# The last token tile in two feature halves, its rows stored alone, its stores from two queues

## The chip, the cores and the metric

The kernel runs on one core of one Trainium2 chip. The metric is device time in microseconds (us), the median over runs. It is 0.6 ms here, and the change touches its last 10 us, so besides the time of the whole program this document uses a second measure, the **tail**: from the start of the first matmul of the last token tiles (called t0; the first instruction that writes the tile `po` at the end) to the end of the span. The tail is worked out from each profile as span minus t0, with the span to three decimals from the trace and t0 to two, so a tail can be off by 0.01.

In the profile lines PE is TensorE (matmuls), DVE VectorE, ACT ScalarE, SP SyncE and POOL GpSimd. A `q` after the name, as in SPq, marks the queue in which that engine issues instructions; SP and ACT issue the stores of this document. A store *lands* when its completion is signalled.

## The reference

```python
def reference(x, w_tok1, w_tok2, w_ch1, w_ch2):     # cut to what matters
    x = np.fft.fft(np.fft.fft(x, axis=1), axis=2).real            # x: 8 x 3008 x 256
    h = np.maximum(x.transpose(0, 2, 1) @ w_tok1, 0.0) @ w_tok2   # mixes tokens
    u = x + h.transpose(0, 2, 1)
    h2 = np.maximum(u @ w_ch1, 0.0) @ w_ch2                       # mixes channels, 256 -> 1536 -> 256
    return u + h2
```

The change lies in the last product, `relu(u @ w_ch1) @ w_ch2`, in the addition of `u`, and in the stores, for the last 512 tokens of the program alone.

## The kernel before

A chunk holds 512 tokens, as four tiles of 128 (`ks` = 0 to 3; I call them tile 0 to tile 3). `c1` is the relu'd hidden layer of the chunk, `wc2` the second weight, `rt` the residual `u` with tokens on partitions (its upper features stored in reverse order, hence `turned_`), `osb` the result before it is stored. `ps_out` and `ps_mm` give tiles of 128 x 512 fp32 in PSUM, the memory into which the matmuls write. Like the prediction, I call the place of one such tile a bank.

```python
    lower, upper, turned_ = slice(0, P), slice(P, D), slice(D, P, -1)     # P = 128, D = 256

    def residual(eng, o, x, y):
        eng.tensor_tensor(out=o, in0=x, in1=y, op=AT.add)

    def mm2(b, c, c1, ks, box):
        # ... (other chunks go another way; osb allocated at ks == 0)
        last = c + 1 == NCH
        final = last and b + 1 == BB
        if final:
            box["po"] = (ps_out, ps_mm)[ks % 2]("po")
        # ...
        po = box["po"]
        o = D * (ks % 2)
        for ct in range(NCT if n else 0):                                  # NCT = 12
            nc.tensor.matmul(po[0:n, o:o + D], lhsT=c1[:, ct, ks * P:ks * P + n],
                             rhs=wc2[:, ct, :],
                             start=(ct == 0), stop=(ct == NCT - 1))
        if ks % 2 == 1 or final:
            # ... two additions, lower and upper features, for each tile of the final chunk
                for j, p in ((lower, lower), (upper, turned_)):
                    residual(nc.vector, osb[r, ks_, j], src[r, k0:k1, j], rt[r, ks_, p])
        first = 2 if final and ks == 3 else 0
        if ks == 3 or (final and ks == 1):
            for i in range(2):
                nk = min(ks + 1, 3 if last and (i or n == 0) else 4)
                eng = nc.scalar if i and final else nc.sync
                eng.dma_start(
                    out=dram(out_t, (b * S + 8 * c + i + 2 * first) * D,
                             [[NQ * D, 64], [2 * D, nk - first], [1, D]]),
                    in_=osb[64 * i:64 * i + 64, first:nk, :])
            if ks == 3 and last and b % 2:
                nc.sync.dma_start(
                    out=dram(out_t, ((b - 1) * S + NQ - 1) * D, [[NQ * D, 64], [1, D]]),
                    in_=osb[64:P, 3, :])
```

In the final chunk the lower 64 partitions of tile 3 are rows of the last batch, the upper 64 the tail rows of the batch before it. So before the change the end has three stores: tiles 2 and 3 for partitions 0 to 63 (128 KB, queue of SP), tile 2 for partitions 64 to 127 (64 KB, queue of ACT), and the tail rows (64 KB, SP).

## Time and profile before

| | before |
|---|---|
| time | 607.27 us, median of 3 runs (607.2 to 607.56) |
| span of the profiled run, granted clock | 605.8 us, 0.999 |
| TensorE busy | 97% of the span |
| t0 | 595.87 us |
| tail | 9.98 us |

The page of the kernel before: its first line, the busy line of its part 1 (busy us, share of the span, instructions) and the engine shares of its part 4, the chain of waits.

```profile
span 605.8 us, 15712 instructions
PE 589.6 (97%) x6323; PEld 421.7 (70%) x6323; DVE 454.3 (75%) x1022; ACT 437.0 (72%) x983; POOL 148.5 (25%) x234
PE 86%; DMA 6%; DVE 5%; issue 1%; ACT 1%; POOL 1%; DVEq 0%; POOLq 0%
```

TensorE is the bound, and only what happens after it has stopped, or what makes it stop, can be gained in the tail. The timeline of the kernel before, at its end. Columns: start, duration, engine, line, operation, output and input, count, and in brackets the idle time before it with what ended it.

```profile
595.87 5.40 PE L834 MATMUL po<-wc,c 128*128 128x256 f16 x48
...
599.20 3.22 SPq L852 DMA_DIRECT2D out_dram<-osb  x2
599.20 1.81 ACTq L852 DMA_DIRECT2D out_dram<-osb  x2
599.99 0.49 DVE L762 TENSOR_TENSOR osb<-po,rt 128x128 f32<-128x128 f32 x2 [0.82 <-PE po L834]
601.30 0.49 DVE L762 TENSOR_TENSOR osb<-po,rt 128x128 f32<-128x128 f32 x2 [0.82 <-PE po L834]
602.47 0.60 SPq L857 DMA_DIRECT2D out_dram<-osb  x1
```

TensorE runs without a gap to 601.27; the two additions of tile 3 end at 601.79; SP's second store in the merged line, asked for alone, is

```profile
601.82 0.60 SPq L852 DMA_DIRECT2D out_dram<-osb  x1
```

It holds the queue for 0.6 us, so the last one, at 602.47, starts 0.65 later. Those two in the view of DMA issues of the kernel before, from 601.5 us on (size, us from issue to landing):

```profile
out_dram<-osb SPq DMA_DIRECT2D x1, 128.0 KB, 2.4
out_dram<-osb SPq DMA_DIRECT2D x1, 64.0 KB, 2.1
```

The last landing is at 602.47 + 2.1, about 604.56, and the closing sequence takes the rest of the span, about 1.3 us.

In another chunk, VectorE reads one half of `px` while the next matmuls write its other half. The timeline of the kernel before, near 60 us:

```profile
59.63 0.42 DVE L762 TENSOR_TENSOR osb<-px,m 128x256 f32<-128x256 f32 x1
...
60.10 0.83 PE L777 MATMUL px<-wst,sb 128*128 128x128 f16 x12 [0.25 <-DVE osb L762]
```

The addition reads columns 256 to 511 of `px` and ends at 60.05; the matmuls into columns 0 to 255 of it start at 60.10.

### The profile page before, as it was taken

Reading aid. Unit: us, or ns where it says so; the run is one execution under the profiler, and the core shown is the slowest. Engines: PE = TensorE matmul, PEld = TensorE weight load, DVE = VectorE, ACT = ScalarE, POOL = GpSimd, SP = SyncE. Lnnn points to the kernel's source line nnn. Section 1 sums busy time; section 2 is a strip of 40 time slices with the busy share of each in tenths; the row PEclk is TensorE's granted clock in tenths of the full one; section 3 lists DMA queues with packets and bytes.
Section 4 is the critical chain, followed back from the end, with each engine's and each line's share of the span. In section 5 each row is a group of like instructions: output and inputs, shape, how many; then the busy total and the mean of one; then the engine's idle time right before and its main releaser. Section 6 shows DMA issues by size and latency. Waiting matters only on the chain.

```text
span 605.8 us, 15712 instructions
## 1 busy us (share of the span) xinstructions
PE 589.6 (97%) x6323; PEld 421.7 (70%) x6323; DVE 454.3 (75%) x1022; ACT 437.0 (72%) x983; POOL 148.5 (25%) x234
## 2 busy tenths in 40 slices
PE   5999999999999999999999999999999999999996
PEld 3855667666777677666777677766777677766675
DVE  8759699559886698667988689755979666766672
ACT  8775986777677767677767777677776877767772
POOL 7600414112242131402223211411221112111131
PEclk9999999999999999999999999999999999999999
DMA  9995945643457223662519332492231424242423
GB/s 152 210 177 117 176 62 97 141 62 63 53 107 155 57 54 88 134 88 54 97 44 178 70 80 63 83 173 53 54 85 44 86 53 88 55 70 62 87 60 99
DMA packets 86665, 56.53 MB, mean 93 GB/s; under 512 B 54928, under 2 KB 83536, under 8 KB 85840
## 3 DMA queue, kind: packets, MB, share of 16 engines
q1 hardware_dynamic: 78048, 37.84, 32.5%
q0 software_dynamic: 8320, 17.49, 16.9%
q8 instruction: 49, 0.80, 0.5%
q14 instruction: 24, 0.20, 0.1%
q10 hardware_dynamic: 224, 0.20, 0.1%
HBM read 34.98 MB, written 24.64 MB: 98 GB/s over the span
## 4 chain that ended last, share of the span: by engine, by line
PE 86%; DMA 6%; DVE 5%; issue 1%; ACT 1%; POOL 1%; DVEq 0%; POOLq 0%
PE pc L736 37%; PE px L777 23%; PE py L777 9%; PE pu L696 6%; PE po L834 3%; PE pt L604 3%; DMA xm<-in_x_dram,ix 3%; DMA w2s<-in_moe_w_tok_dram 2%; PE pz L509 1%; DMA w1p<-in_moe_w_tok_dram 1%; DVE sb L753 1%; PE pq L636 1%; PE py L636 1%; DVE osb L762 1%; DVE xp L457 1%
## 5 line engine op out<-in xcount | busy, mean ns | idle before, releaser
L739 ACT ACTIVATE c<-pc 128x512 f16<-128x512 f32 (+1 forms) x572 | 295.8, 593 | 38.2 <-PE pc L736 20.6
L762 POOL TENSOR_TENSOR osb<-osb,rt 128x256 f32<-128x256 f32 x84 | 81.2, 966 | 375.6 <-DVE osb L762 359.9
L736 PE MATMUL pc<-ut,wc1p 128*128 128x512 f16 x576 | 140.5, 379 | 0.0
L777 PEld LDWEIGHTS <-c 128*128 128x128 f16 x2016 | 121.4, 98 | 20.7 <-issue 1.3
L736 PE MATMUL pc<-ut,wc1m 128*128 128x512 f16 (+1 forms) x576 | 134.8, 370 | 0.0
L704 DVE TENSOR_TENSOR ut<-pu,yt 128x512 f16<-128x512 f32 (+1 forms) x96 | 64.7, 674 | 52.7 <-PE pu L696 52.7
L777 PEld LDWEIGHTS <-sb 128*128 128x128 f16 x1512 | 89.9, 98 | 12.5 <-DVE sb L753 2.1
L782 ACT ACTIVATE m<-px 128x256 f32<-128x256 f32 x126 | 48.6, 386 | 68.6 <-PE px L777 43.1
L736 PEld LDWEIGHTS <-wc1p 128*128 128x128 f16 x576 | 52.2, 98 | 49.1 <-issue 2.6
L736 PEld LDWEIGHTS <-wc1m 128*128 128x128 f16 x576 | 53.0, 98 | 46.4
L777 PE MATMUL px<-wst,c 128*128 128x128 f16 x1008 | 70.8, 219 | 0.2 <-DVE c L753 0.2
L777 PE MATMUL px<-wc,c 128*128 128x128 f16 x1008 | 63.1, 219 | 0.0
L753 DVE TENSOR_TENSOR sb<-sb,c 128x768 f16<-128x768 f16 x84 | 50.3, 599 | 2.9
L305 ACT ACTIVATE z<-pz 128x480 f16<-128x480 f32 (+1 forms) x60 | 40.0, 671 | 16.9 <-PE pz L509 11.0
L753 DVE TENSOR_TENSOR sb<-c 128x768 f16<-128x768 f16 x84 | 49.8, 592 | 2.3 <-ACT c L739 2.3
L762 DVE TENSOR_TENSOR osb<-py,m 128x256 f32<-128x256 f32 x84 | 35.2, 419 | 20.8 <-ACT m L782 18.9
L696 PE MATMUL pu<-w2p,uu 128*128 128x512 f16 (+1 forms) x168 | 50.0, 379 | 0.0
L753 DVE TENSOR_TENSOR sb<-c,sb 128x768 f16<-128x768 f16 x84 | 47.2, 561 | 0.0
L753 DVE TENSOR_TENSOR c<-c 128x768 f16<-128x768 f16 x84 | 46.6, 555 | 0.0
L590 DVE SCALAR_TENSOR_TENSOR w<-alt,pw 128x131 f16<-128x131 f16 x84 | 29.3, 350 | 18.2 <-ACT w L305 17.6
L643 DVE TENSOR_TENSOR yt<-py,qs 128x512 f16<-128x512 f32 x48 | 30.9, 686 | 15.7 <-ACT qs L639 14.8
L777 PE MATMUL py<-wst,sb 128*128 128x128 f16 x504 | 35.3, 219 | 1.7 <-DVE sb L753 1.7
(184 smaller groups left out, 681.0 us busy)
## 6 DMA issues: line engine op xcount, KB each, us to landing
out_dram<-osb SPq DMA_DIRECT2D x83, 256.0 KB, 3.7
xp<-in_x_dram POOLq DMA_DIRECT2D x16, 272.0 KB
out_dram<-osb SPq DMA_DIRECT2D x11, 192.0 KB, 3.2
xp<-in_x_dram POOLq DMA_DIRECT2D x16, 127.5 KB
rt<-ut SPq DMA_TRANSPOSE x96, 3.6
w2s<-in_moe_w_tok_dram POOLq DMA_DIRECT2D x1, 1504.0 KB
w1p<-in_moe_w_tok_dram POOLq DMA_DIRECT2D x4, 192.0 KB
wc<-in_moe_w_ch_dram POOLq DMA_DIRECT2D x1, 768.0 KB
```

Of the source, the lines that this page charges most:

```text
L305: nc.scalar.activation(out=out_, in_=in_, func=AFT.Copy)
L590: nc.vector.scalar_tensor_tensor(out=w[:, g, 0:131], in0=alt[:], scalar=pw[:, 131:132], in1=pw[:, 0:131], op0=AT.mult, op1=AT.add)
L604: nc.tensor.matmul(pt[:, o:o + n], lhsT=hw[:, g, th * P:th * P + P], rhs=w[:, g, f:f + n], start=(g == 0), stop=(g == NG - 1))
L643: nc.vector.tensor_tensor(out=yt[:, h, CW * c:CW * c + CW], in0=py[:], in1=qs[:], op=op)
L696: nc.tensor.matmul(pu[:, 0:n], lhsT=uu[:, th, int(minus), h, :], rhs=w2_cols(b, c)[:, th], start=(th == 0), stop=(th == 1))
L704: nc.vector.tensor_tensor(out=ut[:, h, 0:n].rearrange("p (a b) -> p a b", b=64), in0=pu[:, 0:n].rearrange("p (b a) -> p a b", b=64), in1=y ...
L736: nc.tensor.matmul(pc[:, 0:n], lhsT=wc[:, h, ct * P:(ct + 1) * P], rhs=ut[:, h, 0:n], start=(h == 0), stop=(h == 1))
L739: nc.scalar.activation(out=c1[:, ct, 0:n], in_=pc[:, 0:n], func=AFT.Relu)
L753: nc.vector.tensor_tensor(out=o, in0=x, in1=y, op=op)
L762: eng.tensor_tensor(out=o, in0=x, in1=y, op=AT.add)
L777: nc.tensor.matmul(o[:, t], lhsT=a(k)[:, f:f + P], rhs=w(k), start=(first and t == 0 and k == 0), stop=(k == HC - 1), skip_group_check=True)
L782: nc.scalar.activation(out=m[:, i], in_=pa[:, 0], func=AFT.Copy)
```

## The change

Intent: overlap half of the last addition with matmuls, send tile 2's rows ahead so that the last stores are small, and issue the last stores side by side.

```diff
-        for ct in range(NCT if n else 0):
-            nc.tensor.matmul(po[0:n, o:o + D], lhsT=c1[:, ct, ks * P:ks * P + n],
-                             rhs=wc2[:, ct, :],
-                             start=(ct == 0), stop=(ct == NCT - 1))
-        if ks % 2 == 1 or final:
+        w = P if final and ks == 3 else D
+        for d in range(0, D if n else 0, w):
+            for ct in range(NCT):
+                nc.tensor.matmul(po[0:n, o + d:o + d + w],
+                                 lhsT=c1[:, ct, ks * P:ks * P + n],
+                                 rhs=wc2[:, ct, d:d + w],
+                                 start=(ct == 0), stop=(ct == NCT - 1))
+            if final and ks == 3:
+                j, p = ((lower, lower), (upper, turned_))[d // w]
+                residual(nc.vector, osb[:, 3, j], po[:, o + d:o + d + w], rt[:, 3, p])
+        if ks % 2 == 1 and not final or final and ks < 3:
 ...
-        first = 2 if final and ks == 3 else 0
-        if ks == 3 or (final and ks == 1):
+        first = ks if final and ks > 1 else 0
+        if ks == 3 or (final and ks):
             for i in range(2):
                 nk = min(ks + 1, 3 if last and (i or n == 0) else 4)
+                if nk == first:
+                    continue
 ...
             if ks == 3 and last and b % 2:
-                nc.sync.dma_start(
+                (nc.scalar if final else nc.sync).dma_start(
```

After it, tile 2 leaves as two stores of 64 KB, and tile 3 as two stores of 64 KB, each pair from SP and ACT.

## The prediction

> **What bounds the kernel.** The page: TensorE busy 97% of 605.8 us, full clock; the chain of waits is 86% PE. The change touches only the last microseconds, so it can save only tenths of a microsecond.
>
> **The tail before (timeline, chain, windows view).** The 48 matmuls of the last token tiles (128x256, 0.11 us apart) run from 595.87 to 601.27 without a gap. DVE adds tile 3's residual in two instructions, 601.30 to 601.79 (0.28 us each, 0.49 the pair). SP issues the store of two rows (128 KB) at 601.80, which holds its queue 0.6 us, and only then, at 602.47, the 64 KB store of the previous batch's tail rows. They land 2.4 and 2.1 us after issue: 604.2 and 604.57. Packets run from 603.0 to about 604.1. An end sequence takes the span to 605.8. So the exposed tail is matmul, DVE pair, serial issue, last landing.
>
> **What the change does.**
> 1. Tile 3: 12 matmuls of 256 columns become 24 of 128. The chain shows twelve 128-column matmuls in 0.67 us, so 1.34 against 1.33: no work saved or added.
> 2. The first half's residual leaves the end; DVE after the last matmul shrinks from 0.49 to 0.28: -0.21.
> 3. But both halves lie in one PSUM bank, and DVE reads the first half before PE may write the second. The Trainium skill, "PSUM — Partial Sum Buffer", section "PSUM bank collisions raise a hardware error", says a different address in the same bank still collides, and its rule is to guard by bank. This trace agrees that the program waits so: at 60.10 a matmul into one half of px had waited 0.25 us for a DVE addition reading the other half (59.63 to 60.05). So PE should stop between halves: DVE start 0.02, addition 0.28, restart 0.05 = 0.35, plus about 0.2 of drain (a 128-column matmul lasts 0.219, they follow every 0.056): about +0.55, PE ends at 601.83 instead of 601.28.
> 4. Net of 2 and 3: DVE finishes near 602.13 instead of 601.79, +0.34.
> 5. Tile 2's rows go out alone at about 600.5, on SP and ACT; one more DMA, SP is free then: no cost.
> 6. The last two stores, 64 KB each, start together from SP and ACT at about 602.14: the second no longer waits 0.67 for SP. The skill, "DMA: Bandwidth & Descriptors", "Issuing engines are not separate DMA queues", says issue from several engines saves only the sequencer's time; here that is the 0.67. As they share the DMA engines, I expect landing 2.1 to 2.4 after issue: 604.25 to 604.55, against 604.57.
>
> Sum: +0.34 from the bank wait, -0.67 serial issue, about +0.15 for two stores moved at once: **about -0.2 us**. The split eats half of what the queues give.
>
> **Predicted: 607.1 us, range 606.4 to 607.8.** Within 2%: 99%; faster and slower 0.5% each.
>
> **What the profile would show.** Right: a PE gap of about 0.35 (released by DVE osb) between the halves; tile 3's additions near 600.7 and 601.85; SP and ACT both issuing at about 602.1; last landing about 604.4. Wrong on 3: no PE gap, last matmul ending at 601.3, one addition ending at 601.6, landing at 603.9, -0.7 in all (606.6). Wrong on 6: the two stores take more than 2.5 to land, or ACT starts late.
>
> **What would make it wrong.** The dependency tracked by columns rather than by bank (-0.5 more); the earlier stores' packets still queued when the last ones come; a different chip, as run-to-run scatter (607.2 to 607.56) is larger than the effect.

## The result, and the profile after

| | before | after |
|---|---|---|
| time, median | 607.24 us (606.57 to 607.56, 4 runs) | 606.63 us (605.65 to 607.04, 4 runs) |
| t0 of the profiled run | 595.87 | 595.26 |
| tail of the profiled run | 9.98 | 9.88 |

The ratio is 0.9989, with a 95% interval of 0.9972 to 1.0006; that is "the same". A ratio here is the mean time of one kernel's fast runs over that of the other's of the same rounds, so not quite the ratio of the medians quoted.

Of the 0.71 us between the two profiled spans (605.85 and 605.14), 0.10 is the tail. The other 0.61 had been gained before the first changed instruction.

The same views of the kernel after. The page:

```profile
span 605.1 us, 15738 instructions
PE 590.3 (98%) x6335; PEld 422.4 (70%) x6335; DVE 455.6 (75%) x1022; ACT 437.0 (72%) x983; POOL 145.9 (24%) x234
PE 88%; DVE 6%; DMA 2%; ACT 2%; issue 1%; DVEq 0%; POOL 0%; POOLq 0%
```

The timeline of its end:

```profile
595.26 4.76 PE L836 MATMUL po<-wc,c 128*128 128x256 f16 x48
...
598.59 3.48 SPq L860 DMA_DIRECT2D out_dram<-osb  x3
598.60 1.82 ACTq L860 DMA_DIRECT2D out_dram<-osb  x2
599.38 0.49 DVE L762 TENSOR_TENSOR osb<-po,rt 128x128 f32<-128x128 f32 x2 [0.82 <-PE po L836]
600.05 0.29 DVE L762 TENSOR_TENSOR osb<-po,rt 128x128 f32<-128x128 f32 x1 [0.18 <-PE po L836]
600.40 0.83 PE L836 MATMUL po<-wc,c 128*128 128x128 f16 x12 [0.38 <-DVE osb L762]
601.26 0.29 DVE L762 TENSOR_TENSOR osb<-po,rt 128x128 f32<-128x128 f32 x1 [0.92 <-PE po L836]
601.59 0.50 ACTq L865 DMA_DIRECT2D out_dram<-osb  x1
```

The first line merges 36 matmuls of 256 columns with the first 12 of 128. Then TensorE stands still for 0.38 us, released by VectorE, whose addition of the first half ends at 600.34. Counted from t0, matmuls end at 5.97 (before 5.40), the last addition at 6.30 (before 5.93), and both last stores are issued at 6.33 (before: 5.95 and 6.60). The view of DMA issues of the kernel after, from 601.5 us on:

```profile
out_dram<-osb SPq DMA_DIRECT2D x1, 64.0 KB, 2.0
out_dram<-osb ACTq DMA_DIRECT2D x1, 64.0 KB, 2.3
```

Unrounded, the last landing is 8.58 after t0, against 8.69 before, and the closing sequence takes 1.30 against 1.29. The trade is as the prediction had it: a later start of the stores against a closer pair.

### The profile page after: what moved, and what is told of

It is laid out like the page before. It is cut to its first block, busy times and chain, and to the rows that moved or that the text cites. A ratio compares the mean times of both kernels' runs of the same rounds, so it can differ in the third digit from the quotient of the medians.

```text
span 605.1 us, 15738 instructions
## 1 busy us (share of the span) xinstructions
PE 590.3 (98%) x6335; PEld 422.4 (70%) x6335; DVE 455.6 (75%) x1022; ACT 437.0 (72%) x983; POOL 145.9 (24%) x234
## 4 chain that ended last, share of the span: by engine, by line
PE 88%; DVE 6%; DMA 2%; ACT 2%; issue 1%; DVEq 0%; POOL 0%; POOLq 0%
PE pc L736 37%; PE px L777 23%; PE py L777 9%; PE pu L696 6%; PE pt L604 4%; PE po L836 4%; DMA xm<-in_x_dram,ix 2%; PE pz L509 1%; DVE sb L753 1%; PE pq L636 1%; PE py L636 1%; DVE osb L762 1%; DVE xp L457 1%; PE pw L588 1%; PE pw L587 1%
## 5 line engine op out<-in xcount | busy, mean ns | idle before, releaser
L762 POOL TENSOR_TENSOR osb<-osb,rt 128x256 f32<-128x256 f32 x84 | 78.6, 936 | 378.8 <-DVE osb L762 363.6
L753 DVE TENSOR_TENSOR sb<-c 128x768 f16<-128x768 f16 x84 | 47.2, 562 | 2.3 <-ACT c L739 2.3
```

The source lines that it names most:

```text
L753: nc.vector.tensor_tensor(out=o, in0=x, in1=y, op=op)
```

## The experiments

My theory was: the split costs time, because TensorE must wait for VectorE on the shared bank; the stores give time, because the second no longer waits for the first one's issue. Rivals: the split is what gains; the gain of the stores comes from their size and not from their queues; and the change also sped up what lies before the tail. All kernels gave correct results.

| run | tile 3 | last stores | TensorE gap in tile 3 | last issue after t0 | its store lands after | tail |
|---|---|---|---|---|---|---|
| before | whole | SP 128 KB, SP 64 KB | none | 6.60 | 2.1 | 9.98 |
| e8, before again | whole | as before | none | 6.60 | 2.1 | 9.97 |
| after | halves, one bank | SP 64, ACT 64 | 0.38 | 6.33 | 2.3 | 9.88 |
| e4, after again | halves, one bank | as after | 0.38 | 6.33 | 2.3 | 9.90 |
| e1 | whole | as after | none | 5.96 | 2.3 | 9.52 |
| e2 | halves, one bank | as before | 0.38 | 6.97 | 2.1 | 10.38 |
| e3 | halves, two banks | as after | none | 5.80 | 2.3 | 9.36 |
| e5 | whole | SP 64, SP 64 | none | 6.49 | 2.1 | 9.78 |
| e6 | whole | SP 128, ACT 64 | none | 5.95 | 2.6 (SP) | 9.88 |
| e7 | quarters, one bank | as after | 0.36, 0.31, 0.32 | 7.25 | 2.2 | 10.79 |
| e9 | 192 + 64, two banks | as after | none | 5.73 | 2.3 | 9.29 |
| e10 | halves, two banks | ACT 64, SP 64 | none | 5.79 | 2.3 (ACT) | 9.36 |
| e11 | halves, two banks | SP 32, ACT 32 | none | 6.15 (ACT; SP 6.23) | 2.1 (ACT) | 9.45 |
| e12, e9 timed | 192 + 64, two banks | as after | none | 5.72 | 2.3 | 9.28 |

Three pairs of profiles of one kernel (before and e8, after and e4, e9 and e12) agree in the tail within 0.02 us, although they come from different jobs (e4 ran on chip 7, e8 on 15, e9 on 3, e12 on 9), so differences of 0.1 can be read from single profiles. Times of whole runs can't show them: those of the kernel before spread over 1.4 us (606.07 to 607.43) within one job of 11 runs.

### e1: only the stores

The kernel after, with tile 3's matmuls and additions as before:

```diff
-        w = P if final and ks == 3 else D
-        for d in range(0, D if n else 0, w):
 ...  (the loop and its residual removed)
+        for ct in range(NCT if n else 0):
+            nc.tensor.matmul(po[0:n, o:o + D], lhsT=c1[:, ct, ks * P:ks * P + n],
+                             rhs=wc2[:, ct, :],
+                             start=(ct == 0), stop=(ct == NCT - 1))
-        if ks % 2 == 1 and not final or final and ks < 3:
+        if ks % 2 == 1 or final:
```

> Only the stores are as after (tile 2 alone, last two stores from SP and ACT); tile 3 is one group of 12 matmuls of 256 columns, as before. Times counted from the first matmul of the last tiles (t0). My theory (the split costs time through the bank wait, the queues give it): matmuls end 5.40 us after t0, both additions by 5.92, both stores issued at 5.93, last landing about 8.2; tail from t0 to the end of the span about 9.45, against 9.98 before and 9.84 after. Rival (the split is what gained): tail no shorter than after, 9.9 or so. The whole time: 606.7 or so beside 607.2, too little for the clock on the wall to settle.

Measured: tail 9.52, time 605.62 us (605.24 to 607.35, 6 runs) against 606.76 of before (606.07 to 607.43, 11 runs); ratio 0.9988, interval 0.9976 to 1.0000. (The 9.84 in the expectation came from the span rounded to one decimal; the tail of after is 9.88.) The end of its timeline, the additions and ACT's last store:

```profile
599.87 0.49 DVE L762 TENSOR_TENSOR osb<-po,rt 128x128 f32<-128x128 f32 x2 [0.82 <-PE po L834]
600.39 0.49 ACTq L859 DMA_DIRECT2D out_dram<-osb  x1
```

The stores alone shorten the tail by 0.46, more than the whole change does. "The split is what gained" falls.

### e2: only the split

The kernel before with the matmul loop of the change, and the stores left as they were:

```diff
+        w = P if final and ks == 3 else D
+        for d in range(0, D if n else 0, w):
+            for ct in range(NCT):
 ...  (as in the change; stores untouched)
```

> Only tile 3 is split in two halves of one bank; the stores are as before (128 KB and then 64 KB, both on SP). My theory: a gap of about 0.38 us between the halves, additions end about 6.29 after t0 instead of 5.92, stores issued at 6.30 and 6.97, last landing about 9.1; tail about 10.35, i.e. 0.37 longer than before. Rival (the split hides one addition and gains its 0.2 us): tail about 9.8.

Measured: tail 10.38, 0.40 longer than before; time 607.2 us (606.23 to 607.25, 5 runs), ratio 1.0006, interval 0.9993 to 1.0019. The gap of 0.38 is there:

```profile
599.70 0.83 PE L836 MATMUL po<-wc,c 128*128 128x128 f16 x12 [0.38 <-DVE osb L762]
```

The two parts add up: -0.46 and +0.40 make -0.06, and the whole change measured -0.10 and, in e4, -0.08 (9.90 against 9.98).

### e3: the halves in two banks

```diff
         for d in range(0, D if n else 0, w):
+            if d:
+                po = ps_out("po")
             for ct in range(NCT):
```

> As after, but the second half of tile 3 goes to another PSUM bank (a second po tile). My theory (the wait is for the bank): no gap on PE, matmuls end 5.40 after t0, the second addition alone follows and ends by 5.71, stores issued at 5.72, last landing about 8.0; tail about 9.25, 0.6 shorter than after and 0.7 shorter than before. Rival (the wait comes from the order of instructions or from splitting as such, e.g. draining between groups): the gap stays and the tail stays near 9.84.

Measured: tail 9.36. The end of its timeline:

```profile
593.96 5.43 PE L838 MATMUL po<-wc,c 128*128 128x256 f16 x60
...
598.76 0.29 DVE L762 TENSOR_TENSOR osb<-po,rt 128x128 f32<-128x128 f32 x1 [0.18 <-PE po L838]
599.43 0.29 DVE L762 TENSOR_TENSOR osb<-po,rt 128x128 f32<-128x128 f32 x1 [0.38 <-PE po L838]
```

The 60 matmuls run in 5.43 us with no gap, while the same instructions in one bank took 5.97. Splitting as such costs nothing; the wait belongs to the shared bank. A bank is one tile here, so these runs do not tell whether the program waits because the bank is shared or because the tile is. The time of whole runs shows none of this (606.97 us, 605.12 to 609.52, ratio 1.0013, interval 0.9997 to 1.0029): the scatter described under e8 is larger. So "a shorter tail" is shown, "a faster program" is not.

### e4: the changed kernel again

No edit.

> The changed kernel itself once more, for the scatter. Both theories: tail from t0 to the end of the span 9.84 within 0.1; the start t0 (595.26 in its profile, 595.87 before) moves by several tenths from run to run for reasons outside the change, so that t0 of this run lies anywhere between 593.5 and 596.5. Rival: if t0 lies near 595.3 again and that of unchanged code near 595.9, the change also works on the code before the tail.

Measured: tail 9.90, t0 594.43, time 606.1 us (605.61 to 607.01, 5 runs), ratio 0.9994, interval 0.9981 to 1.0006. The tail repeats, t0 does not: the same program came to its tail 0.83 us earlier than in the first profile. With e8 below, this decides the rival about the code before the tail.

### e5 and e6: which part of the stores

e5 is e1 with the last two stores both on SP; e6 is the kernel before with one store moved to ACT.

```diff
 e5 against e1:
-                (nc.scalar if final else nc.sync).dma_start(
+                nc.sync.dma_start(
 e6 against before:
-                nc.sync.dma_start(
+                (nc.scalar if final else nc.sync).dma_start(
```

> As e1 (no split, tile 2 stored alone), but the last two stores, 64 KB each, are both issued by SP, one after the other. My theory (the gain of the stores is that the second no longer waits for SP's issue of the first): stores issued at 5.93 and about 6.5 after t0, last landing about 8.6, tail about 9.87, so most of e1's gain of 0.46 against before is gone again. Rival (the gain is that the last stores are smaller and the rest left earlier): tail about 9.5, as e1.

> The kernel before with one word changed: the 64 KB store of the tail rows is issued by ACT instead of SP; the rows of tiles 2 and 3 still leave together, 128 KB on SP. My theory: both issued at 5.93 after t0, landing 2.4 (SP, 128 KB) and 2.3 to 2.5 (ACT), so 8.3 to 8.45; tail about 9.65, i.e. some 0.3 of the 0.46 come from this alone and the smaller SP store is worth the rest. Rival (smaller and earlier stores): tail stays at 9.98.

Measured: e5 tail 9.78 (0.20 shorter than before), e6 tail 9.88 (0.10 shorter). Neither is what I expected: I gave e6 0.3 and it gave 0.1, I gave e5 0.1 and it gave 0.2. Nor does the rival hold, which wanted all of the 0.46 in e5. Each alone gives a part, and both together more than the sum. The view of DMA issues of e6, its last two stores:

```profile
out_dram<-osb SPq DMA_DIRECT2D x1, 128.0 KB, 2.6
out_dram<-osb ACTq DMA_DIRECT2D x1, 64.0 KB, 2.0
```

Both are issued at 5.95. ACT's 64 KB land early, but SP's 128 KB now take 2.6 instead of the 2.4 of before, and they are last, at 8.59. The packets show why: ACT's ran first. The DMA view of e6 lists the packets of one queue alone (queue, packets, MB, share) in each of two stretches, first from 602.3 to 602.6 us, then from 603.0 to 603.5; q10 is ACT's queue, q1 SP's:

```profile
q10 hardware_dynamic: 43, 0.04, 61.2%
```

```profile
q1 hardware_dynamic: 82, 0.07, 62.9%
```

SP's packets began 7.41 after t0 here and 7.21 in before. In e5 nothing travels beside SP's last two stores, and they are issued one after the other:

```profile
604.50 0.49 SPq L854 DMA_DIRECT2D out_dram<-osb  x1
605.04 0.59 SPq L859 DMA_DIRECT2D out_dram<-osb  x1
```

Its 0.20 is made of three pieces: the smaller first store holds SP for 0.49 instead of 0.60 us, so the last issue is 0.11 earlier; the last store lands 0.03 sooner after it; and the closing sequence after the last landing (at 8.55) is 0.06 shorter than before, 1.23 against 1.29 us, for a reason that these runs do not show.

The same numbers read over all runs: one store of 64 KB alone lands in 2.0 (e5's first), one of 128 KB in 2.4 (before); of two issued together the later one lands after 2.1 (32 + 32, e11), 2.3 (64 + 64) or 2.6 us (128 + 64). So what is issued at the end costs roughly 0.3 to 0.4 us per 64 KB, on one queue or two (e11 does not fit: its 64 KB in two stores took 2.1, not 2.0, but its packets are half as large). Moving the tail store to ACT takes 0.65 off its issue, but then 192 KB travel together. Sending tile 2 ahead takes 64 KB off that load; with both on SP the second store still waits 0.54 for the first. Only both changes leave 128 KB issued at once. That sum is an inference from the landings of these profiles; no run varied the bytes alone with everything else held.

### e7: the wait three times

As after, with `w = P // 2`, so four quarters of 64 columns in the one bank (and `p` computed for the reversed upper features).

```diff
-        w = P if final and ks == 3 else D
+        w = P // 2 if final and ks == 3 else D
 ...
-                j, p = ((lower, lower), (upper, turned_))[d // w]
+                j = slice(d, d + w)
+                p = j if d < P else slice(D + P - d, P + D - d - w, -1)
```

> As after, but tile 3 in four quarters of 64 columns in the one bank, so the suspected wait comes three times. My theory: three gaps on PE, each released by DVE's addition, each about 0.31 (an addition of 64 columns should take about 0.22 by the trend of 0.42 for 256 and 0.286 for 128) plus 0.16 to 0.2 of drain, so PE ends 0.8 later than after if 64-column matmuls follow each other at half the 128-column interval of 0.056, and about 1.3 more if they don't get faster than 0.056; tail 10.6 or 11.9. Rival (the wait belongs to the middle of the tile once, e.g. to the change of column address): one gap, tail below 10.2.

Measured: tail 10.79. Three gaps, each released by VectorE:

```profile
599.11 0.51 PE L836 MATMUL po<-wc,c 128*128 128x64 f16 x12 [0.36 <-DVE osb L762]
599.93 0.51 PE L836 MATMUL po<-wc,c 128*128 128x64 f16 x12 [0.31 <-DVE osb L762]
600.76 0.51 PE L836 MATMUL po<-wc,c 128*128 128x64 f16 x12 [0.32 <-DVE osb L762]
```

Matmuls end 6.96 after t0, 0.99 later than after, where I expected 0.8. The wait comes once for each cut inside the bank, as the theory says, and costs about half a microsecond each time: 1.56 over the three against the unsplit 5.40.

### e8: the kernel before again, and where the 0.61 us came from

No edit.

> The kernel before once more, for the scatter of its tail and start. Both theories: tail 9.98 within 0.05. If the 0.61 us by which t0 differed between the two first profiles was scatter of the loads (the wait of PE for DVE sb was 1.7 us in that of before, 0.9 in that of after, 0.5 to 0.6 in the four of the first job), t0 of this run lies at 594.0 to 595.0 when that wait is 0.5 to 0.6, as for the changed kernels. Rival (the change also sped up the code before the tail): t0 near 595.9 again with a wait of 0.5 to 0.6.

Measured: tail 9.97, t0 594.23. The waits of TensorE between 50 and 100 us, the first two lines, of e8 (columns: us in total, times, longest):

```profile
PE pt L604 <- DVE w L590: 0.7, 1, 0.7
PE py L777 <- DVE sb L753: 0.6, 1, 0.6
```

and the first of e9, a changed kernel, in the same view:

```profile
PE py L777 <- DVE sb L753: 1.7, 2, 1.2
```

In the first profile of before that wait was 1.7 as well, and its t0 was 595.87; e9, changed, with 1.7 has 596.04; e8, unchanged, with 0.6 has 594.23. So t0 goes with this wait and not with the change. Its probable source stands in the chain of waits, here one line each of before, after and e4 (start, duration, what):

```profile
30.12 15.43 DMA xm<-in_x_dram,ix
```

```profile
31.26 13.50 DMA xm<-in_x_dram,ix
```

```profile
30.22 13.96 DMA xm<-in_x_dram,ix
```

It is a load of input rows whose end is needed near 45 us. It ended at 45.55 in before (t0 595.87), at 44.76 in after (t0 595.26), at 44.18 in e4 (594.43), and in the others with such a line: e7 44.06 (594.31), e1 44.13 (594.43), e2 44.26 (594.56), e12 44.32 (594.60), e10 44.49 (594.80), e11 44.94 (595.39), e6 45.09 (595.25), e9 45.59 (596.04), e5 46.48 (598.55). A load that ends 1 us later goes with a t0 about 1 us later, in changed and unchanged kernels alike, though not to the tenth (after and e6 have the same t0 with loads 0.33 apart). (e5 lost more; its granted clock between 50 and 100 us was 0.97, where it was 1.00 in the other profiles; its last matmuls took 5.40 us as in before.) In e3 and e8 the chain has no such line, and their t0 are the earliest, 593.96 and 594.23. Why the load ends at a different time in each run these runs do not show.

### e9: an uneven cut, and e12: the same, timed

As e3, but cut at column 192:

```diff
-        w = P if final and ks == 3 else D
-        for d in range(0, D if n else 0, w):
+        cuts = ((0, 192), (192, D)) if final and ks == 3 else ((0, D),)
+        for d, e in cuts if n else ():
+            w = e - d
+            if d:
+                po = ps_out("po")
 ...  (two additions, 128 and 64 columns, after the first cut; one of 64 after the second)
```

> As e3 (two banks), but tile 3 is cut 192 + 64 columns, so that what follows the last matmul is an addition of 64 columns (0.22 in e7) and not of 128 (0.29). My theory (everything after the last matmul is exposed, one for one): matmuls end at most 0.05 later than in e3, the last addition 0.07 shorter: tail 9.3, at best 9.25, against 9.36 in e3. Rival (the two additions of the first 192 columns, 0.29 and 0.22, hold DVE so that the last one starts late, or the 64-column matmuls are limited by their weight loads): tail no shorter than 9.36.

> The kernel of e9 (two banks, 192 + 64 columns, last two stores from two queues), which has the shortest tail so far, timed in five rounds. Tail 9.29 again within 0.05, against 9.98 before: 0.69 us, 0.1% of the whole. If the start behaves as in the other runs, a ratio of about 0.999, with an interval of some 0.1% to each side that may or may not reach 1; the theory makes no claim beyond that. If its tail is off by more than 0.1, the tails of single profiles are not to be trusted as I have used them.

Measured: tails 9.29 and 9.28, the shortest of all, 0.07 under e3: what is taken from after the last matmul comes off one for one. In time e12 has 605.82 us (605.23 to 607.93, 6 runs) against 606.39 of before (606.13 to 607.18, 11 runs), ratio 0.9996, interval 0.9983 to 1.0009. This version ends better than both kernels by 0.7 and 0.6 us of tail; five rounds do not show that in the time of the whole program.

### e10: the queues of the last two stores swapped

```diff
-                eng = nc.scalar if i and final else nc.sync
+                eng = nc.scalar if final and i != (ks == 3) else nc.sync
 ...
-                (nc.scalar if final else nc.sync).dma_start(
+                nc.sync.dma_start(
```

> As e3, but of the last two stores SP issues the tail rows and ACT the last batch's rows. In after, SP's store landed 2.0 us after issue and ACT's 2.3, and the later one ends the span. Theory one (it is the queue: two stores issued at once go out one behind the other, SP's first): ACT 2.3 again, SP 2.0; tail 9.36 as in e3. Theory two (it is the rows: partitions 64 to 127 or their place in memory land later): SP 2.3, ACT 2.0; tail 9.36 too, as the issue is at the same time.

Measured: tail 9.36, and again SP's store lands after 2.0 and ACT's after 2.3, though their rows have changed places. So the 0.3 does not belong to the rows. It does not belong to ACT's queue as such either: in e6 ACT's 64 KB landed first, after 2.0. In every profile with a pair issued together at the end, the store whose issue ended first landed first: SP's by 0.01 in most, and ACT's by 0.09 in e6, where SP's larger store held its queue longer. In e11 ACT's issue began 0.08 before SP's and ended 0.01 after it, and ACT's landed last. That is a pattern of these profiles; no run tested it. Swapping the rows leaves no room to gain.

### e11: each half stored at once

As e3, and inside the loop, after each addition:

```diff
+                for i, eng in enumerate((nc.sync, nc.scalar)):
+                    eng.dma_start(
+                        out=dram(out_t, ((b - i) * S + NQ - 1) * D + d, [[NQ * D, 64], [1, P]]),
+                        in_=osb[64 * i:64 * i + 64, 3, j])
```

> As e3, but each half of tile 3's features is stored as soon as it has been added, from both queues, so that the last two stores are 32 KB each in rows of 512 bytes instead of 64 KB in rows of 1 KB. The queues are free in between: the first halves are issued at about 5.1 after t0 and hold their queues 0.5, the last at about 5.80. My theory (what is left after issue is partly the packets of the two stores themselves, as between 64 KB, 2.0, and 128 KB, 2.4): landing 1.9 and 2.1, tail 9.2 against 9.36 in e3. Rival (the 2.0 is a fixed time, and smaller rows cost as much per packet): tail 9.36 or longer. The whole time is still under the scatter of the start: 605.0 to 606.5 beside 606.8.

Measured: tail 9.45, worse than e3; time 606.61 us (605.82 to 607.12, 5 runs), ratio 0.9997, interval 0.9983 to 1.0010. The smaller stores do land sooner (1.8 and 2.1 against 2.0 and 2.3), but I was wrong that the queues are free. SP's last store was issued at 6.23 and ACT's at 6.15 after t0, though VectorE was done as early as in e3 (5.76), where both were issued at 5.79. For ACT the store of the first half held the queue, from 5.26 to 6.06, 0.8 us instead of the 0.5 I had assumed. For SP it was something else, which the view of its waits in e11 shows:

```profile
SPq L846 <- DMA out_dram<-osb: 0.4, 1, 0.4
```

SP waited 0.4 us for an earlier store to land. The compiled program uses eight completion semaphores in rotation, and the semaphore of this store was last used by a 256 KB store of the chunk before, issued at 2.47 after t0 and landing 3.7 later, at 6.17. None of the profiles of the other kernels that I looked at (after, e1, e2, e3, e5, e6, e7, e10) has such a wait before a store. So more stores in the tail are not free even where the queues are: 0.36 was lost at ACT's issue, 0.13 came back at its landing, another 0.13 in a shorter closing sequence (1.17 against 1.30 us, reason not shown), and the tail is 0.1 longer.

## Why the prediction was right or wrong

- **The whole (right, within the range).** Predicted 607.1 (606.4 to 607.8), "the same"; measured 606.63, "the same". But of the 0.6 us between the two medians of these four runs each, the change explains about 0.1. That the median lies in the range is in good part luck and says little: the range is 1.4 us wide, and the median of the kernel before, 607.24, lies in it too. The rest has the size of the scatter of the start (e4, e8), and the interval of the ratio includes 1.
- **Step 3, the bank wait (right).** Predicted: a gap of 0.35 and matmuls ending about 0.55 later. Measured: 0.38, and 0.57 later (5.97 against 5.40). e3 takes the gap away with another bank (which is another tile too), e7 gives it three times. The Trainium skill, "PSUM — Partial Sum Buffer", section "PSUM bank collisions raise a hardware error", tells to guard PSUM by bank and quadrant and not by address (both halves here use all 128 partitions, so the bank alone decides); this program waits so, and its own trace showed that before the change, at 60.10 us.
- **Steps 2 and 4, the net of the split (right).** Predicted +0.34 at VectorE's end; measured +0.37 in after, and +0.40 of tail in e2.
- **Step 6, the last issue (right in direction, a little large).** Predicted: the last issue 0.33 earlier, landing 0.15 later, -0.2 in all. Measured: 0.27 earlier (6.33 against 6.60), landing 2.3 instead of 2.1, -0.10 and -0.08 of tail in two profiles. Term by term the sum was +0.34, -0.67 and +0.15; unrounded, after against before gives +0.37, -0.64 and +0.16, which is -0.11 at the last landing. Each term was off by at most 0.03, all three in one direction.
- **What failed: the attribution in the sum.** The prediction put "-0.67 serial issue" on the two queues and said of storing tile 2 alone only "no cost". e6 has the queue move alone and gains 0.10; e5 has tile 2 alone and gains 0.20; only both give 0.46. The prediction had a term for two stores of 64 KB moved at once, +0.15, and it was right for them; it did not see that the term is larger while tile 2's rows still travel with them: 128 KB on SP took 2.4 alone, 2.6 beside ACT's 64 KB. The -0.67 came out nearly right for the pair because both parts were in the change. The skill's "DMA: Bandwidth & Descriptors", "Issuing engines are not separate DMA queues", says that several issuing engines share the same DMA engines and save only the issue; e6 agrees, more than I had reckoned.

## What to carry to other kernels

Before an output tile is cut to overlap its evacuation with matmuls, look which PSUM bank, or tile, the pieces lie in: in one tile each cut made TensorE wait for the reader (0.4 us of tail lost here), in two tiles, each in a bank of its own, the same cut gained (9.52 in e1, 9.36 in e3). At the end of a program, time what has still to be moved when the last result is ready, not the number of queues: splitting over two queues helped little until fewer bytes were left. And when a change can be worth only tenths of a microsecond, measure the stretch that it touches, from an event that it does not move: here whole runs scattered by over 1 us, while the tail repeated within 0.02.

## What the Trainium skill lacked or had wrong

- "DMA: Bandwidth & Descriptors" gives, for DMAs issued from GpSimd, a fit of 2.0 us plus bytes over 436 GB/s, by which 64 KB more would cost 0.15 us (an estimate from that fit). For these stores of 64 rows issued from SP and ACT, 64 KB more cost 0.4 us: 2.0 against 2.4 for one store alone (e5, before).
- The same page's "Issuing engines are not separate DMA queues" calls the issue time "usually small relative to the DMA itself". Here one issue held its queue 0.5 to 0.6 us, of 2.0 to 2.6 from issue to landing, and 0.8 us for ACT's first half store in e11.
- I found no page that says which of two stores issued at once lands first, or by how much. ACT's landed 0.3 us after SP's in after, e1, e3, e9, e10 and e12, whichever rows they carried (e10), but 0.65 us before SP's in e6, where SP's was twice as large and its issue ended 0.09 later.
- "PSUM — Partial Sum Buffer" states the rule on banks and gives no price for keeping it. Here a cut inside a bank stopped TensorE for 0.38 us (128 columns) or 0.31 to 0.36 us (64 columns), and cost 0.40 us of tail.
